# Attention with a routed expert layer: the gate's exponential, the third pair's decay rows, and the first pair's cast order

## The chip, the cores and the metric

The kernel runs on one core of a Trainium2 chip. The metric is the device time of one execution in microseconds (us). The engines are TensorE (PE, its weight load PEld), VectorE (DVE), ScalarE (ACT), GpSimd (POOL) and SyncE (SP, which issues most of the loads and stores). They run side by side, each through its own queue in order, and wait for each other by semaphores.

## What is computed

Causal attention with a decay per position for 8 batches of 8 heads (576 positions, 64 wide), whose output is sent through a layer of 8 experts, one for each token:

```
scores = scale * np.matmul(q, k.transpose(0, 1, 3, 2))
log_f = np.log(np.clip(f, 0.0001, 1.0))
cum = np.cumsum(log_f, axis=-1)
decay = cum[:, :, :, None] - cum[:, :, None, :]
scores = np.where(causal, -1000000000.0, scores + decay)
attn = np.exp(scores - scores.max(-1)) / sum
x = (attn @ v) as 4608 rows of 512
logits = x @ w_gate
expert_idx = np.argmax(logits, axis=1)
logits_shift = logits - logits.max(-1, keepdims=True)
probs = np.exp(logits_shift);  probs /= probs.sum(-1, keepdims=True)
out[token] = probs[expert_idx] * (relu(x @ w1[expert]) @ w2[expert])
```

## The kernel before

Attention works on pairs of heads: 32 pairs, numbered 0 to 31 here and in the code (n), four to a batch, so pair 0 is the first, pair 2 the third. A pair's q and k come as one tile of 128 partitions (two heads of q, then two of k: 1280 and 1152 columns), called `raw`. Every float is split into a rounded high part and the rest, and a score is a sum of two matmuls: the first multiplies the high parts (`qk1`, written qk in the profile), the second the rests together with the decay (`q2` and `k2`, 68 partitions; rows 64 to 67 hold the cumulated decay and constants). PE takes these two in that order for every tile, so a late `q2` or `k2` stops PE with the first matmul done.

The loop runs over n, and each n has seven steps i. In a step PE makes scores of pair n (`s_tiles`, `s_joint`), then transposes of the exponentials of pair n-1 (`t_tiles`, `t_one`, `t_joint`); in step 1 it also makes the products with v for pair n-2 (`av`). DVE reads each score bank, adds the mask and takes a row minimum (`s_red`, L339), ACT makes the exponential (`s_exp`, L346), and both copy transposes out of PSUM. The order of each engine's instructions is that of the loop (`order.pin`).

For pairs 0 and 1 the casts and splits are spread over ACT, DVE and POOL (`first_q`, `first_k`, `second_q`, `second_k`). From pair 2 on POOL does most of it: a cast of q, the rest of head 2's q (`q_parts`, in step 5 two pairs ahead), then a copy of q and the rest of k (`copies`, step 2 one pair ahead), four instructions in a row.

Loads are issued by SP in program order (`sp_dma`). A load's semaphore is one of eight, taken in turn, and the built program makes a load wait, where nothing later has done so, until the load eight places ahead of it has landed. The decay lies in the tile `cw` in SBUF. Pairs 0 and 1 get their decay rows straight from it (`c_rows`, five small transfers a pair); `cw` is also written to DRAM (`cq`, `ck`), and from pair 2 on the rows come from there (`load_c`, two transfers).

When a batch's four pairs are done, its routing runs between the steps of the next pairs. For batch b the logits are finished in pair 4b+6 (`fin_logits`, parts 0 and 1 in steps 3 and 4), and step 1 of pair 4b+7 runs `softmax` and `expert` (pairs 7, 11, up to 31): DVE takes the maximum and the shifted logits `w.sh`, which lie in the PSUM bank `ps_r` (pr in the profile), ACT takes their exponential (`ex`, L811), DVE compares them (`cand`, L814) and builds a one-hot table (`ohb`, L824), from which PE makes ranks in step 3 (L840). The last batch does the same while the first expert is under way. After attention comes the expert layer, a long run of matmuls (L1093, L1116).

Of the kernel before, what the change touches and what calls it, by code (L numbers as in the profile page):

```python
# [8 lines left out]
F32 = mybir.dt.float32  # L9
F32R = mybir.dt.float32r  # L10
# [3 lines left out]
AF = mybir.ActivationFunctionType  # L14
ALU = mybir.AluOpType
# [4 lines left out]
P = 128  # L20
S = 576
# [60 lines left out]
def psum(pool):  # L82
    return pool.tile([P, 512], F32, name="ps", tag="ps")
# [11 lines left out]
def attention_all(c, tc, qkT, va, vb, f, wgd, x_dram, batch_done, more_consts, extra):  # L95
# [6 lines left out]
    nc = tc.nc  # L102
    V = nc.vector
    B = qkT.shape[0]
    NH = B * H
    JW = S // 2
    QW = 1280
# [7 lines left out]
    with ExitStack() as st:  # L115
# [4 lines left out]
        sm, sp = c.sm, c.sp  # L120
# [18 lines left out]
        def sp_dma(out, in_):  # L139

            return tc.keep_in_program_order(nc.sync.dma_start(out, in_))

        def load_pair(n, parts=(0, 1)):

            if n not in raws:
                pool, tag = (c.xap, "xa") if n % 3 == 2 else (c.wp, "R")
                raws[n] = pool.tile([P, QW + 2 * S], F32, name="raw", tag=tag)
            raw = raws[n]
            b, p = divmod(n, NPAIR)
            cols = ((0, QW), (QW, QW + 2 * S)) if n < 3 else ((0, QW + 2 * S),)  # L150
            for c0, c1 in [cols[i] for i in parts if i < len(cols)]:
                for h in range(2):
                    last = sp_dma(raw[h * HD : (h + 1) * HD, c0:c1], qkT[b, p, :, c0:c1])
            return last
# [23 lines left out]
        halves = ((slice(0, NPR), slice(512, S)), (slice(NPR, NH), slice(S, 640)))  # L178
        for hs, cs in halves:
            scan(cum[hs, cs], fr[hs, 512:S], cum[hs, 511:512])  # L180
        cw = sp.tile([NH, 2, 640], F32R, name="cw", tag="aT")
        cwf = cw.bitcast(F32)
        V.tensor_copy(cw[:, 0, :], cum)
        V.tensor_tensor(cw[:, 1, :], cum, cwf[:, 0, :], ALU.subtract)
# [4 lines left out]
        NQ = 2  # L189
# [73 lines left out]
        def first_q(n):  # L263
            qk1, raw, q2 = operands(n), raws[n], Q2s[n]
            pin(nc.scalar.copy(qk1[:, 0:QW], raw[:, 0:QW]))
            if n == 1:
                nc.gpsimd.tensor_copy(q2[0:64], raw[0:64, 0:QW])

        def first_k(n):
            qk1, raw, q2 = ops[n][0], raws[n], Q2s[n]  # L270
            pin(nc.scalar.copy(qk1[:, QW:], raw[:, QW:]))  # L271
            if n == 0:
                pin(nc.scalar.copy(q2[0:64], raw[0:64, 0:QW]))

        def second_q(n):
            pin(lo(V, n, ops[n][0][64:128, 0:QW], 64, 0, QW))
# [30 lines left out]

        def c_rows(n, j):

            q2c, k2c = Q2s[n][64:66].bitcast(F32), K2s[n][66:68].bitcast(F32)  # L310
            r = cwf[j * NPR + n : j * NPR + n + 1]
            if j == 0:
                sp_dma(k2c[:, 0, :], r[:, :, 0:S])
                sp_dma(q2c[:, 0:640], r)
            else:
                sp_dma(k2c[:, 1, 0:512], r[:, :, 0:512])
                sp_dma(k2c[:, 1, 512:], r[:, :, S:640])
                sp_dma(q2c[:, 640:], r)
# [227 lines left out]
                    ))  # L546
                nc.scalar.copy(gT[:, q0:q1], g[:, 0 : q1 - q0])

        def fin_logits(b, part):
            rinv = rinvs[b]  # L550
            if part == 0:
                lgs[b] = (c.ps_r[:, 0:40].rearrange("p (t e) -> p t e", e=8),
                          sm.tile([P, 5, 8, 8], F32, name="gq", bufs=1))
            lg, gq = lgs[b]
            pg = psum(fin_bank[0])
            tiles = (0, 1, 2, 3) if part == 0 else (4,)
            for i, t in enumerate(tiles):
                note(nc.tensor.transpose(
                    pg[:, P * i : P * i + P], gT[:, P * t : P * t + P], c.ident
                ))  # L560
            for i, t in enumerate(tiles):
                V.tensor_tensor(
                    gq[:, t],
                    pg[:, P * i : P * i + P].rearrange("q (h e) -> q e h", e=16)[:, 0:8, :],
                    rinv[:, t, :].unsqueeze(1).to_broadcast([P, 8, 8]), ALU.mult,
                )
            if part == 1:
                V.tensor_reduce(lg, gq, AX.X, ALU.add)
# [4 lines left out]
        def fin_tasks(b):  # L573

            (softmax, expert, gate, rank, slot, hi, lo, table), after = batch_done(
                b, lambda: lgs[b][0]
            )
            fx = [lambda t=t: fin_x(b, t, b == B - 1 and t > 0) for t in range(5)]  # L580
            lg = [lambda p=p: fin_logits(b, p) for p in range(2)]
            g = NPAIR * b + 6
            if b == B - 1:
                return dict(fx=fx, lg=lg, softmax=softmax, expert=expert, gate=gate,
                            rank=rank, slot=slot, hi=hi, lo=lo, table=table,
                            logits=lambda: fin_gate(b))
            r = [(0, 2, fx[0]), (0, 3, lg[0]), (0, 4, lg[1]), (1, 1, softmax),
                 (1, 1, expert), (1, 3, rank)]
            if b < B - 2:
                r += [(2, 1, gate), (2, 1, slot), (2, 2, fx[1]), (2, 3, fx[2]),  # L590
                      (3, 1, hi), (3, 1, lo), (3, 2, fx[3]), (3, 3, fx[4]), (3, 5, table)]
            else:
                r += [(2, 1, gate), (2, 1, slot), (2, 2, fx[1]), (2, 3, hi), (2, 3, lo),
                      (2, 4, fx[2]), (2, 5, fx[3]), (2, 6, fx[4]), (3, 0, table)]
            for dn, i, f in r + after:
                tasks.setdefault((g + dn, i), []).append(f)
# [36 lines left out]
        c_rows(1, 0)  # L633
        c_rows(1, 1)
        load_pair(2)

        sp_dma(cq[:, :, 0], cwf[0:NPR])
        sp_dma(cq[:, :, 1], cwf[NPR:NH])
        sp_dma(ck[:, :, 0, :], cwf[0:NPR, :, 0:S])
        sp_dma(ck[:, :, 1, 0:512], cwf[NPR:NH, :, 0:512])  # L640
        sp_dma(ck[:, :, 1, 512:], cwf[NPR:NH, :, S:640])
        tasks, c.later, order = {}, [], InOrder(tc)
        c.note = note
        for n in range(NP + 2):
# [8 lines left out]
            for i in range(7):  # L653
                for x in c.later:
                    x[0] -= 1
                while c.later and c.later[0][0] <= 0:
                    c.later.pop(0)[1]()
                if n == 0:
                    if i == 0:
                        first_q(1)  # L660
                        late_consts()
                    elif i == 2:
                        second_q(1)
                    elif i == 3:
                        first_k(1)
                    elif i == 5:
                        second_k(1)
                elif n + 1 < NP:
                    if i == 0:
                        load_c(n + 1)  # L670
                        if n == 1:
                            load_pair(3)
                    elif i == 2:
                        copies(n + 1)
                if i == 5 and n + 2 < NP:
                    q_parts(n + 2)
                if i == 5 and n == 2:
                    load_gate()
                if i == 3 and n < NP:
                    load_v(n)  # L680
                if i == 2 and 0 < n < NP - 3:
                    c.mark = load_pair(n + 3)
                s_, e_ = ss[i] if ss else (None, None)
                if s_:
                    step(s_)
                if ts_:
                    step(ts_[i])

                if e_:
                    e_()  # L690
                if i == 1 and 0 < n and n + 1 < NP:
                    k_first(n + 1)
                if i == 1 and 2 <= n:
                    step(lambda: av(n - 2))
                    av_out()


                    fb, fp = divmod(n - 2, NPAIR)
                    if fp == 0 and 1 <= fb:
                        step(lambda: fin_gate(fb - 1))  # L700
                        fin_tasks(fb - 1)
                    elif fp == NPAIR - 1 and fb == B - 1:
                        todo = fin_tasks(fb)

                fin_bank[0] = (ps_v, ps_m)[i % 2]
                for f in tasks.pop((n, i), []):
                    step(f)
                at = {(0, 1): 0, (1, 0): 1, (1, 1 if b == B else 4): 2}.get((p, i))
                if n >= NPAIR and at is not None:
                    fin_sums(b - 1, at)  # L710
                if (n, i) == (NP, 0):
                    scores.close()
                for f in extra(n, i):
                    step(f)
                order.pin()
                if (n, i) == (NP + 1, 1):
                    break
# [12 lines left out]
E = 8  # L730
# [56 lines left out]
def route_stages(c, tc, b, lg_of, last):  # L787
# [14 lines left out]
    def softmax():  # L802
# [3 lines left out]
        w.sh = tokens(40, 5)  # L806
        V.tensor_tensor(w.sh, lg, bc(mx), ALU.subtract)

    def expert():
        w.ex = rs.tile([P, 5, E], F32, name="ex")  # L810
        nc.scalar.activation(w.ex, w.sh, AF.Exp)  # L811

        cand = rs.tile([P, 5, E], F32, name="cand")
        V.scalar_tensor_tensor(  # L814
# [606 lines left out]
```

## Time and profile before

| | |
|---|---|
| median of 3 runs | 862.28 us (861.4 to 862.44) |
| the profiled execution, time | 861.09 us |
| its span, first to last instruction | 859.3 us |
| PE busy | 816.6 us, 95% |
| DVE, ACT, POOL busy | 54%, 50%, 45% |
| mean granted clock of TensorE | 0.990 |

The profile gives, for one execution, each engine's busy time; a list of waits (which engine stood idle ahead of which line, and what released it); a timeline with starts and durations; and the busy time, granted clock and transfers in chosen stretches. Attention takes the span up to about 380 us, the experts the rest. An engine that isn't the one waited for may idle at no cost, so the waits of the busiest engine are read first.

### The profile page before, as it was taken

The page shows a single profiled execution, that of the slowest core. Times are in us where ns is not written, and L with a number is a line of the kernel's source. Part 1 is how long each engine was busy: PE and PEld are TensorE (multiplying, and loading weights), DVE is VectorE, ACT ScalarE, POOL GpSimd, SP SyncE. Part 2 cuts the span into 40 slices and gives each one's busy share as a digit, 9 for nine tenths or more (in the row PEclk, how much of TensorE's full clock was granted, in tenths as well). Part 3 has the DMA queues.
Part 4 walks back from the last instruction along what each step waited for, and adds up shares of the span by engine and source line. Part 5 has one row for each costly group of instructions (what it writes and reads, how often), then busy time and mean ns, then how long its engine had stood idle before and what let it go on. Part 6 is the DMA issues. An engine that isn't in the chain of part 4 may idle for free. (4 is left out here: it accounts for less than half of the span.)

```text
span 859.3 us, 15386 instructions
## 1 busy us (share of the span) xinstructions
PE 816.6 (95%) x5664; PEld 713.9 (83%) x5664; DVE 462.9 (54%) x1427; ACT 432.3 (50%) x1108; POOL 388.2 (45%) x310
## 2 busy tenths in 40 slices
PE   4899999999999999999999999999999999999992
PEld 3778787878787878788899899898898998988982
DVE  7656767676767778655472544445425444354200
ACT  6888888888888989855221223122122221231210
POOL 7798696969696978651530230312203103101010
PEclk9999999999999999999999999999999999999996
DMA  7997676767676765522651450533415405324000
GB/s 170 223 191 162 163 178 164 183 150 187 152 184 154 176 152 146 175 93 86 191 190 50 147 170 21 189 109 119 149 46 171 143 4 183 104 74 132 1 37 17
DMA packets 39893, 114.65 MB, mean 133 GB/s; under 512 B 6847, under 2 KB 8895, under 8 KB 36104
## 3 DMA queue, kind: packets, MB, share of 16 engines
q1 hardware_dynamic: 32776, 93.70, 42.2%
q0 software_dynamic: 6400, 19.93, 6.4%
q8 instruction: 46, 0.75, 0.4%
q14 instruction: 31, 0.25, 0.1%
q10 hardware_dynamic: 640, 0.01, 0.0%
HBM read 94.07 MB, written 20.55 MB: 133 GB/s over the span
## 5 line engine op out<-in xcount | busy, mean ns | idle before, releaser
L1116 PE MATMUL ps<-w,hh 128*128 128x512 f32 x640 | 199.3, 395 | 0.0
L346 ACT ACTIVATE sc<-sc,nmx 128x512 f32<-128x512 f32 (+4 forms) x288 | 167.3, 582 | 34.7 <-DVE nmx L339 34.2
L1124 POOL DMA_INDIRECT out<-y,si_fast x37 | 42.4, 1146 | 312.1 <-ACT y L1123 283.4
L339 DVE CUSTOM_DVE_ANT_0 sc<-ps,mask 128x512 f32<-128x512 f32 (+4 forms) x288 | 129.2, 479 | 63.7 <-PE ps L332 63.0
L1098 ACT ACTIVATE hh<-ps 128x384 fp32r<-128x384 f32 (+1 forms) x128 | 56.1, 438 | 194.5 <-PE ps L1093 194.5
L1093 PE MATMUL ps<-xa,w 128*128 128x384 f32 x768 | 145.1, 337 | 0.1
L332 PE MATMUL ps<-qk 128*128 128x288 f32 (+4 forms) x384 | 126.9, 361 | 16.0 <-ACT qk L271 10.8
L1099 DVE SCALAR_TENSOR_TENSOR hl<-ps,hh 128x384 fp32r<-128x384 f32 (+1 forms) x128 | 62.4, 489 | 146.2 <-ACT hh L1098 145.0
L1116 PEld LDWEIGHTS ps<-w,hh 128*128 128x128 f32 x640 | 118.2, 188 | 23.6
L1093 PEld LDWEIGHTS ps<-xa,w 128*128 128x128 f32 x768 | 132.7, 188 | 1.4 <-DVE hl L1099 0.2
L1116 PE MATMUL ps<-w,hl 128*128 128x512 f32 x320 | 124.8, 395 | 0.0
L332 PE MATMUL ps<-k,q 68*128 68x288 f32 (+4 forms) x384 | 105.7, 323 | 5.2 <-POOL k L249 3.8
L249 POOL TENSOR_TENSOR k<-raw,qk 64x1152 fp32r<-64x1152 f32 x30 | 79.4, 2647 | 53.7 <-ACT qk L291 49.0
L1093 PE MATMUL ps<-xb,w 128*128 128x256 f32 x768 | 101.8, 283 | 0.0
L1093 PEld LDWEIGHTS ps<-xb,w 128*128 128x128 f32 x768 | 98.9, 189 | 2.8
L470 PE MATMUL ps<-aT,va_t 128*64 128x256 f32 (+3 forms) x896 | 94.6, 354 | 0.0
L1123 ACT ACTIVATE y<-ps,g_fast 128x512 f32<-128x512 f32 x37 | 25.5, 689 | 136.6 <-PE ps L1116 130.7
L391 ACT COPY aT<-ps 128x512 f32<-128x512 f32 (+1 forms) x156 | 83.2, 534 | 14.1 <-PE ps L400 6.8
L332 PEld LDWEIGHTS ps<-qk 128*128 128x128 f32 x384 | 69.6, 195 | 23.6 <-ACT qk L271 10.8
L249 POOL TENSOR_TENSOR qk<-raw,qk 64x1280 fp32r<-64x1280 f32 x30 | 87.8, 2928 | 2.4
L470 PEld LDWEIGHTS ps<-aT,va_t 128*64 128x64 f32 x896 | 58.9, 137 | 29.2 <-issue 6.1
L969 DVE CAST w<-wraw 128x1024 fp32r<-128x1024 f32 x56 | 39.2, 707 | 80.3 <-PE ps L1116 54.3
(161 smaller groups left out, 1133.2 us busy)
## 6 DMA issues: line engine op xcount, KB each, us to landing
raw<-in_qkT SPq DMA_DIRECT2D x58, 608.0 KB
wraw<-in_w SPq DMA_DIRECT2D x63, 512.0 KB
va_t<-in_va SPq DMA_DIRECT2D x32, 256.0 KB
x_dram<-row SPq DMA_DIRECT2D x32, 256.0 KB
raw<-in_qkT SPq DMA_DIRECT2D x6, 320.0 KB
raw<-in_qkT SPq DMA_DIRECT2D x6, 288.0 KB
vb<-in_vb SPq DMA_DIRECT2D x32, 32.0 KB
x_dram<-row SPq DMA_DIRECT2D x8, 128.0 KB
```

What stands on the lines that cost most here:

```text
L249: return eng.tensor_tensor(o, raws[n][p0 : p0 + 64, c0:c1], ops[n][0][p0 : p0 + 64, c0:c1].bitcast(F32), ALU.subtract,)
L332: note(nc.tensor.matmul(out, ql[:, q0 : q0 + P], kl[:, j, k0 : k0 + kw], start=(i == 0), stop=(i == last),))
L339: V.tensor_tensor_reduce(scs[n][:, dst : dst + src.shape[1]], src, m, -0.125, init, ALU.add, ALU.min, nms[n][:, col : col + 1],)
L346: nc.scalar.activation(x, x, AF.Exp, bias=nms[n][:, col : col + 1], scale=-1.0, accum_out=acc)
L391: nc.scalar.copy(dst, src)
L470: c.last_av = note(nc.tensor.matmul(pv[j * HD : (j + 1) * HD, q0 - qa : qb - qa], l, r, start=(blk == 0), stop=(blk == nb - 1),))
L969: V.tensor_copy(w[:, 0], raw)
L1093: c.note(nc.tensor.matmul(ph[:, 0:n], w[:, wi, fs], x[:, xi, kt, :], start=(k == 0), stop=(k == 3 * KT - 1),))
L1098: nc.scalar.activation(hh[:, ft, :], ph[:, 0:n], AF.Relu)
L1099: nc.vector.scalar_tensor_tensor(hl[:, ft, :], ph[:, 0:n], 0.0, hh[:, ft, :].bitcast(F32), ALU.max, ALU.subtract,)
L1116: c.note(nc.tensor.matmul(py, hi_[:, ft, ms], w[:, wi], start=(ft + k == 0), stop=(ft == FT - 1 and k == 2),))
L1124: nc.gpsimd.indirect_dma_start(out=self.out, out_offset=bass.IndirectOffsetOnAxis(ap=si[:, s : s + 1], axis=0), in_=y, in_offset=None, bou ...
```

## The change

There are four edits.

1. Gate. `softmax` subtracts the maximum a second time, into a new SBUF tile `shs`, and ACT's exponential reads that in place of `w.sh` in PSUM. Part 1 of `fin_logits` moves from step 4 of pair 4b+6 to step 0 of pair 4b+7 and takes the bank `ps_m`. This is done for batches 0 to 6; the last batch gets the second subtraction alone.
2. Pair 2's decay rows come straight from `cw`, as those of pairs 0 and 1, and are issued ahead of pair 3's raw data; the writes to `cq` and `ck` come behind that. `cw` is taken from the pool of `xT`.
3. Pair 2's raw data is loaded whole, in two transfers in place of four.
4. Pair 0's `q2` cast goes ahead of its k cast on ACT, and the k casts of pairs 0 and 1 are made in two halves of 576 columns.

```diff
-            cols = ((0, QW), (QW, QW + 2 * S)) if n < 3 else ((0, QW + 2 * S),)
+            cols = ((0, QW), (QW, QW + 2 * S)) if n < 2 else ((0, QW + 2 * S),)
...
-        cw = sp.tile([NH, 2, 640], F32R, name="cw", tag="aT")
+        cw = c.xp.tile([NH, 2, 640], F32R, name="cw", tag="xT")
...
             pin(nc.scalar.copy(qk1[:, 0:QW], raw[:, 0:QW]))
-            if n == 1:
-                nc.gpsimd.tensor_copy(q2[0:64], raw[0:64, 0:QW])
...
-            pin(nc.scalar.copy(qk1[:, QW:], raw[:, QW:]))
             if n == 0:
                 pin(nc.scalar.copy(q2[0:64], raw[0:64, 0:QW]))
+            else:
+                nc.gpsimd.tensor_copy(q2[0:64], raw[0:64, 0:QW])
+
+        def first_k(n):
+            qk1, raw = ops[n][0], raws[n]
+            for c0, c1 in ((QW, QW + S), (QW + S, QW + 2 * S)):
+                pin(nc.scalar.copy(qk1[:, c0:c1], raw[:, c0:c1]))
...
-            r = [(0, 2, fx[0]), (0, 3, lg[0]), (0, 4, lg[1]), (1, 1, softmax),
+            r = [(0, 2, fx[0]), (0, 3, lg[0]), (1, 0, lambda: fin_logits(b, 1, ps_m)), (1, 1, softmax),
                  (1, 1, expert), (1, 3, rank)]
...
                 elif n + 1 < NP:
-                    if i == 0:
+                    if i == 0 and n > 1:
                         load_c(n + 1)
-                        if n == 1:
-                            load_pair(3)
+                    elif i == 0:
+                        c_rows(2, 0)
+                        c_rows(2, 1)
+                        load_pair(3)
+                        c_writes()
...
         V.tensor_tensor(w.sh, lg, bc(mx), ALU.subtract)
 
+        w.shs = rs.tile([P, 5, E], F32, name="shs")
+        V.tensor_tensor(w.shs, lg, bc(mx), ALU.subtract)
...
-        nc.scalar.activation(w.ex, w.sh, AF.Exp)
+        nc.scalar.activation(w.ex, w.shs, AF.Exp)
```

On DVE, from the end of pair 6 to the maximum in pair 7's step 1, before (ISA rows are `s_red`, gq and pr<-gq are part 1 of the logits, mx the maximum; the subtraction and `cand` follow):

```order
L562 TENSOR_TENSOR gq<-ps,rinv 128x64
L568 TENSOR_REDUCE pr<-gq 128x40
L339 ISA sc,nmx<-ps,mask 128x288
L339 ISA nmx 128x1
L389 COPY aT<-ps 68x2x64
L339 ISA sc,nmx<-ps,maskj,nmx 128x288
L339 ISA nmx 128x1
L339 ISA sc,nmx<-ps,mask 128x512
L339 ISA nmx 128x1
L339 ISA sc,nmx<-ps,mask 128x512
L339 ISA nmx 128x1
L805 TENSOR_REDUCE mx<-pr 128x5
```

The same place on DVE in the changed kernel:

```order
L341 ISA sc,nmx<-ps,mask 128x512
L341 ISA nmx 128x1
L564 TENSOR_TENSOR gq<-ps,rinv 128x64
L570 TENSOR_REDUCE pr<-gq 128x40
L341 ISA sc,nmx<-ps,mask 128x512
L341 ISA nmx 128x1
L811 TENSOR_REDUCE mx<-pr 128x5
L813 TENSOR_TENSOR pr<-pr,mx 128x40
L816 TENSOR_TENSOR shs<-pr,mx 128x40
L823 SCALAR_TENSOR_TENSOR cand<-pr,iota5m 128x40
```

Part 1 of the logits has moved behind the first `s_red` of pair 7, and one subtraction stands ahead of `cand`; everything behind keeps its order.

On SP's queue, from pair 2's raw data on, before (q and k with cw or cq, ck are decay rows):

```order
L141 DMA raw<-in_qkT 64x1280 x2
L141 DMA raw<-in_qkT 64x1152 x2
L141 DMA cq<-cw 64x1x640 x2
L141 DMA ck<-cw 64x1x576
L141 DMA ck<-cw 64x1x512
L141 DMA ck<-cw 64x1x64
L141 DMA va_t<-in_va 128x512
L141 DMA vb_174<-in_vb 64x128
L141 DMA q_0_142<-cq 2x1280
L141 DMA k_0_144<-ck 2x1152
L141 DMA raw<-in_qkT 64x2432 x4
```

The same stretch of SP's queue in the changed kernel, whose next rows are the rest of ck and pair 4's raw data:

```order
L141 DMA raw<-in_qkT 64x2432 x2
L141 DMA va_t<-in_va 128x512
L141 DMA vb_174<-in_vb 64x128
L141 DMA k_0_144<-cw 2x1x576
L141 DMA q_0_142<-cw 2x1x640
L141 DMA k_0_144<-cw 2x1x512
L141 DMA k_0_144<-cw 2x1x64
L141 DMA q_0_142<-cw 2x1x640
L141 DMA raw<-in_qkT 64x2432 x2
L141 DMA cq<-cw 64x1x640 x2
L141 DMA ck<-cw 64x1x576
```

Pair 2's raw data is two rows in place of four, the five writes to DRAM stand behind pair 3's raw data and ahead of pair 4's, and the rows of pair 2 no longer come through DRAM.

## Rows read from the trace of the kernel before

**Rows 1.** The page, busy time of PE, share and instructions.

```profile
PE 816.6 (95%) x5664; PEld 713.9 (83%) x5664; DVE 462.9 (54%) x1427; ACT 432.3 (50%) x1108; POOL 388.2 (45%) x310
```

**Rows 2.** Waits of PE, whole span: who <- released by: us, times, longest.

```profile
PE ps L332 <- ACT qk L271: 10.8, 1, 10.8
PE ps L332 <- DVE nmx L339: 4.5, 7, 0.7
PE ps L332 <- POOL k L249: 3.8, 2, 2.6
PE pr L840 <- DVE ohb L824: 2.7, 6, 0.4
PE ps L400 <- DVE aT L389: 1.9, 1, 1.9
...
PE ps L332 <- DMA q<-cw: 1.4, 1, 1.4
```

**Rows 3.** PE in a stretch: from:to, length, busy, granted clock, transfers' share, GB/s.

```profile
60.00:360.00 300.00, 292.17 (x2534) 1.00 0.69 166
```

**Rows 4.** Waits of DVE, whole span.

```profile
DVE cand L814 <- ACT ex L811: 24.5, 8, 3.5
```

**Rows 5.** Timeline, pair 7: start, us, engine line operation [idle before <- releaser].

```profile
88.99 0.34 PE L332 MATMUL ps<-k,q 68*128 68x384 f32 x1
...
89.88 0.22 ACT L811 ACTIVATE ex<-pr 128x40 f32<-128x40 f32 x1
...
90.13 0.20 DVE L814 SCALAR_TENSOR_TENSOR cand<-pr,iota5m 128x40 f32<-128x40 f32 x1 [3.47 <-ACT ex L811]
...
91.25 0.55 DVE L339 CUSTOM_DVE_ANT_0 sc<-ps,mask 128x384 f32<-128x384 f32 x1
...
91.39 0.20 PE L840 MATMUL pr<-ohb,trib 128*128 128x48 bf16 x1 [0.44 <-DVE ohb L824]
...
95.27 0.47 PE L332 MATMUL ps<-qk 128*128 128x512 f32 x1 [0.71 <-DVE nmx L339]
```

**Rows 6.** Timeline, pair 31, the seventh batch routed.

```profile
359.74 0.62 ACT L346 ACTIVATE sc<-sc,nmx 128x384 f32<-128x384 f32 x1 [1.26 <-DVE nmx L339]
...
361.71 0.29 DVE L389 COPY aT<-ps 128x128 f32<-128x128 f32 x1 [0.91 <-ACT aT L391]
...
364.02 0.69 DVE L389 COPY aT<-ps 128x512 f32<-128x512 f32 x1
...
364.76 1.00 PE L400 MATMUL ps<-ident,sc 128*128 128x128 f32 x4 [1.94 <-DVE aT L389]
```

**Rows 7.** PE in two stretches, columns as in rows 3.

```profile
364.00:369.00 5.00, 4.24 (x24) 0.66 0.02 5
39.00:43.00 4.00, 1.41 (x10) 1.00 1.06 228
```

**Rows 8.** Timeline of ACT and PE, pair 0.

```profile
10.62 1.25 ACT L273 CAST q<-raw 64x1280 fp32r<-64x1280 f32 x1
...
10.76 0.80 PE L332 MATMUL ps<-qk 128*128 128x512 f32 x1 [10.76 <-ACT qk L271]
...
12.92 0.77 PE L332 MATMUL ps<-k,q 68*128 68x512 f32 x1 [1.36 <-DMA q<-cw]
```

**Rows 9.** Timeline of POOL: its first instructions for pairs 2 and 3.

```profile
21.55 1.25 POOL L287 CAST qk<-raw 128x1280 fp32r<-128x1280 f32 x1 [3.47 <-DMA raw<-in_qkT]
...
33.86 1.25 POOL L287 CAST qk<-raw 128x1280 fp32r<-128x1280 f32 x1 [4.12 <-DMA raw<-in_qkT]
```

**Rows 10.** Timeline of PE: the second matmul of pairs 2 and 3.

```profile
29.80 0.50 PE L332 MATMUL ps<-k,q 68*128 68x512 f32 x1 [1.25 <-POOL k L249]
...
42.05 0.50 PE L332 MATMUL ps<-k,q 68*128 68x512 f32 x1 [2.60 <-POOL k L249]
```

**Rows 11.** Timeline of SP's queue: raw data of pairs 2, and 3 with 4.

```profile
16.10 2.44 SPq L141 DMA_DIRECT2D raw<-in_qkT  x4
...
25.72 2.43 SPq L141 DMA_DIRECT2D raw<-in_qkT  x4
```

More of the change, by code (lines that the diff above doesn't have):

```diff
@@ L265, in first_q @@
             pin(nc.scalar.copy(qk1[:, 0:QW], raw[:, 0:QW]))
-            if n == 1:
+            if n == 0:
+                pin(nc.scalar.copy(q2[0:64], raw[0:64, 0:QW]))
+            else:
                 nc.gpsimd.tensor_copy(q2[0:64], raw[0:64, 0:QW])
         def first_k(n):
-            qk1, raw, q2 = ops[n][0], raws[n], Q2s[n]
-            pin(nc.scalar.copy(qk1[:, QW:], raw[:, QW:]))
-            if n == 0:
-                pin(nc.scalar.copy(q2[0:64], raw[0:64, 0:QW]))
+            qk1, raw = ops[n][0], raws[n]
+            for c0, c1 in ((QW, QW + S), (QW + S, QW + 2 * S)):
+                pin(nc.scalar.copy(qk1[:, c0:c1], raw[:, c0:c1]))
         def second_q(n):
@@ L308, in c_rows @@
         def c_rows(n, j):
-            q2c, k2c = Q2s[n][64:66].bitcast(F32), K2s[n][66:68].bitcast(F32)
+            q2c, k2c = (t[n % NQ][r : r + 2].bitcast(F32) for t, r in ((Q2s, 64), (K2s, 66)))
             r = cwf[j * NPR + n : j * NPR + n + 1]
@@ L547, in fin_gate, with fin_logits @@
                 nc.scalar.copy(gT[:, q0:q1], g[:, 0 : q1 - q0])
-        def fin_logits(b, part):
+        def fin_logits(b, part, bank=None):
             rinv = rinvs[b]
@@ L554, in fin_logits @@
             lg, gq = lgs[b]
-            pg = psum(fin_bank[0])
+            pg = psum(bank or fin_bank[0])
             tiles = (0, 1, 2, 3) if part == 0 else (4,)
@@ L635, in attention_all, with c_writes @@
         load_pair(2)
[L637 to L641, printed above, removed]
+        def c_writes():
+            sp_dma(cq[:, :, 0], cwf[0:NPR])
+            sp_dma(cq[:, :, 1], cwf[NPR:NH])
+            sp_dma(ck[:, :, 0, :], cwf[0:NPR, :, 0:S])
+            sp_dma(ck[:, :, 1, 0:512], cwf[NPR:NH, :, 0:512])
+            sp_dma(ck[:, :, 1, 512:], cwf[NPR:NH, :, S:640])
         tasks, c.later, order = {}, [], InOrder(tc)
@@ L681, in attention_all @@
                 if i == 2 and 0 < n < NP - 3:
-                    c.mark = load_pair(n + 3)
+                    load_pair(n + 3)
                 s_, e_ = ss[i] if ss else (None, None)
```

## The prediction

> **What bounds the kernel now.** I read the page first: PE is busy 816.6 us [rows 1] of a span of 859.3, so time can only be won where PE stands idle, and the list of PE's waits says where that is. Of the 43 us of idle time, 10.8 lie ahead of the first matmul, 1.4 behind it, 3.8 are waits for POOL's `k2`, and the rest of what is listed are waits for DVE: 4.5 us for score minima, 2.7 for the one-hot table, 1.9 for a transpose copy [rows 2]. A stretch that leaves out start and end confirms it: from 60 to 360 us PE is busy 292.2 of 300 us, at a granted clock of 1.00 (2.4 GHz), so 7.8 us is all that can be won there by removing waits [rows 3]. The list of DVE's waits then names what makes DVE late: `cand` waits for ACT's `ex` 24.5 us in 8 waits of up to 3.5 us, in the pairs 7, 11 to 31 and after the last batch [rows 4]. Both instructions only read the tile in PSUM. DVE has nothing to wait for in its own data; it waits because the built program orders it behind ACT's read.
>
> **The gate, six batches.** In pair 7 DVE stands idle 3.47 us up to 90.13, when ACT has reached `ex` at 89.88, behind its other work of that step; the one-hot table follows, and only at 91.25 does DVE take the score bank that PE had finished with the matmul of 88.99 to 89.33. PE waits 0.44 us for the table and, three steps later, 0.71 us for a bank that DVE has not read yet [rows 5]. With `shs` in SBUF, `cand` has no wait for ACT in the built program, so DVE can do `cand` and the table from 86.7 on (90.13 less 3.47), all of it inside the idle 3.47 us, and is ready for the bank at 89.4, some 1.8 us sooner. That is more than 0.44 and 0.71. ACT's copies, behind which DVE waits in the next two steps, take their turn after DVE's minima and move up with them. The second subtraction is one more DVE instruction of the size of `cand`, 0.20 us [rows 5], and part 1 of the logits, moved by one step, is no more work; both lie in what was idle. PE's transpose for it stands a few instructions later in a queue that runs on. What is late next is nothing on DVE: it then waits for PE. So the six table waits, 2.7 us, and six of the seven waits for minima, 4.3 us (the seventh lies in pair 0), should go [rows 2]. With the smaller stops between them the ceiling is the 7.8 us of [rows 3]; I take **-7.3 us**.
>
> **The gate, seventh batch.** Pair 31 holds more work on DVE and ACT, and the stop there is larger. ACT waits 1.26 us for a minimum at 359.74, DVE waits for ACT's copy until 361.71, does its last copy of the step at 364.02, and PE, which waited 1.94 us, goes on at 364.76 [rows 6]. Without the stall ACT's exponential starts at once, so this chain moves up by its 1.26 us, and PE's wait shrinks to some 0.7 us: -1.3 us. The gap has a second price. From 364 to 369 us the granted clock is 0.66 on the mean [rows 7], which is 3.4 us at the lower level (1.2 GHz) and the rest at the upper, after PE had stood idle. Five us at 0.66 lose 1.7 us of PE's work; some of it is the idle time itself, so 1.5 us. A gap of 0.7 us leaves the clock alone, as the 0.71 us waits did in [rows 3]. Together **-2.8 us**; bounds 0 (the gap stays) and -3.6 (gap and clock loss both vanish).
>
> **First pair.** ACT's `q2` cast, now behind the k cast, takes 1.25 us from 10.62; the first matmul starts at 10.76, but the second waits until 12.92 for the decay rows, which have their own transfer [rows 8]. Their place in SP's queue does not change. With `q2` first and half of k behind it PE may start some 0.5 us earlier and then waits that much longer. The second halves of the k casts cost at most another instruction's start on ACT; what hides them is this wait and, behind it, the wait of pair 2. **0 us**; if the cover were gone, -0.5.
>
> **Pair 2, the third.** POOL starts on it at 21.55, when the two transfers with its q have landed, and on pair 3 at 33.86 [rows 9]. PE's second matmul of pair 2 starts at 29.80 after a wait of 1.25 us for POOL, 8.2 us after POOL's start, and that of pair 3 at 42.05 after 2.60 us [rows 10]. Now POOL's first cast waits for whole transfers with q and k. How late these land the trace shows for the same form: pair 3's were issued from 25.72 on [rows 11] and POOL began at 33.86, 8.1 us later. Pair 2's are issued from 16.10 on [rows 11], so POOL begins near 24.2, **2.7 us later than before**, and PE's second matmul of pair 2 starts near 32.4. The bounds are 23 (the second half of the bytes at a faster rate) and 25. The decay rows, five small transfers, go out when PE has done with pair 0 near 20 us, far ahead of 32.4.
>
> Pair 3 gains what pair 2 loses. In the built program its raw data waits until the first half of the eight loads ahead, pair 2's raw data, has landed, and so is issued near 24.2 rather than 25.72, when the decay rows had come back from DRAM; in 8.1 us it is there, at 32.4, just when POOL is done with pair 2. POOL then needs another 8.2 us, to 40.6. PE needs 9.65 us from the second matmul of pair 2 to its stop in pair 3 (29.80 to 42.05 less 2.60 [rows 10]) and so comes to pair 3 at 42.1: no wait is left, and PE is where it was, at 42.05. The 2.60 us wait of pair 3 has become a longer wait of pair 2: **+0.1 us**. The rows of pair 3 still come through DRAM, behind writes that now stand behind its raw data; the bytes ahead of them are the same, and the loads don't stand idle as long for them, so they should land ahead of 42; up to 1.5 us is the bound if they don't. The moved writes also stand ahead of pair 4's raw data, which POOL wants at 40.6 in place of 42.
>
> **The longer gap.** PE then stands idle 1.25 + 2.7 = 3.9 us ahead of 32.4. After 2.60 us of idling the granted clock was 1.00 (39 to 43 us), after 1.94 us it fell [rows 7]. So a gap's length alone does not decide, but 3.9 us is longer than either, and I expect the fall to the lower level: a price between 0 and 1.7 us, and I take **+1.4**, near the row where it fell, as part of the low stretch may lie in the gap. The Trainium skill, page "TensorE: Matmul & The Clock Gate", section "Part 1: The HAM clock gate", says that half rate is the default that activity lifts, and that the check is "free-running — it doesn't reset when your kernel starts". By this rule one and the same gap can cost or not from run to run, and the sum would be 1.4 us better in some runs; the two gaps of [rows 7] agree with it.
>
> **Sum.** -7.3 - 2.8 + 0 + 0.1 + 1.4 = -8.6 us. Against the profiled execution (861.09 us) that is 852.5. The median is 1.2 us above that execution, so I forecast **853.7 us**.
>
> **Rivals.**
> The clock does not fall after the longer gap. For it: it didn't after 2.60 us. Against: this gap is half as long again. 862.28 - 10.0 = 852.3 us.
> The waits go by half. DVE is free earlier, but the waits for minima three steps later stay, since ACT's copies hold DVE up there (0.91 us in [rows 6]). For it: that wait is there in the row. Against: ACT itself waits for DVE 2 us ahead of it, and moves up when DVE does. 4.3 us stay: 858.0 us.
> The change doesn't do what it says: `cand` gets another late wait, DVE stalls as before, and only pair 2's cost is left, 862.28 + 1.5 = 863.8 us. Against it stands the built order, in which `cand` follows the two subtractions on its own engine with no wait for ACT.
> The loads become the bound, and the kernel is slower. From 39 to 43 us the transfers' share is 1.06 and PE waits [rows 7]; SP now stands at the small rows of pair 2 until PE releases them, and later at pair 3's rows until the DRAM writes have landed. If the loads then stand idle for longer than they do before by X, each pair to about 60 us comes later by X. The decision point is X = 10.3 us, where -8.6 + 10.3 passes +1.7; at 12 us the time is 865.7. Against it: eight loads are under way at a time, and the longest wait for a load in [rows 9] is 4.12 us.
>
> **How the numbers follow.** The forecast has 0.50 (853.7), the unchanged clock 0.25 (852.3), half the waits 0.13 (858.0), no effect 0.04 (863.8), the loads 0.02 (865.7), and 0.06 is left for gains beyond my ceiling, near 850. A measurement of this kernel tells 0.2%, 1.7 us, from no change. Faster: 0.50 + 0.25 + 0.13 + 0.06 = 0.94; same 0.04; slower 0.02. The range goes from 851.0 (no clock loss, all of the 7.8 us) to 858.0.
>
> **What would show it.** `cand` with no wait for ACT; no idle time of PE ahead of the ranks and of step 0 of pairs 8, 12 up to 28; from 60 to 360 us PE busy to within 1 us of the stretch; a gap near 0.7 us in pair 31 at a clock of 1.00; POOL's first cast of pair 2 near 24.2, PE's wait ahead of pair 2 near 3.9 us with a low clock behind it, none ahead of pair 3. I am wrong if pair 3 still waits for POOL or its rows, or if the stops in pairs 7 to 31 only move.

## The result and the profile after

| | before | after |
|---|---|---|
| median | 862.31 us (861.4 to 862.44) | 849.28 us (848.61 to 850.01) |
| ratio | | 0.9851, 95% interval 0.9834 to 0.9868 |
| profiled execution, time and span | 861.09, 859.3 us | 850.01, 848.3 us |
| mean granted clock | 0.990 | 0.987 |

The change saves 13.0 us where 8.6 were forecast. 849.28 lies below the range (851.0 to 858.0), in the case that had 0.06, gains beyond the ceiling.

The first line of the page of after, beside [rows 1]:

```profile
PE 812.9 (96%) x5664; PEld 715.0 (84%) x5664; DVE 464.3 (55%) x1435; ACT 432.9 (51%) x1110; POOL 391.7 (46%) x310
```

PE executes the same 5664 matmuls and is busy 3.7 us less, although its clock was a little lower. That already says that "busy" held something other than work. The list of PE's waits in after (who, released by: us in total, times, longest), beside [rows 2]:

```profile
PE ps L334 <- POOL k L250: 3.3, 1, 3.3
PE ps L334 <- POOL qk L250: 2.0, 1, 2.0
PE ps L334 <- DMA q<-cw: 1.6, 1, 1.6
PE ps L402 <- DVE aT L391: 1.0, 1, 1.0
...
PE ps L334 <- DVE nmx L341: 0.3, 1, 0.3
```

The table waits (2.7 us in 6) are gone, those for minima are down from 4.5 us in 7 to one of 0.3. DVE's 24.5 us of waiting for `ex` [rows 4] are gone too. Pair 7 in after, DVE and ACT, beside [rows 5]:

```profile
89.42 0.19 DVE L823 SCALAR_TENSOR_TENSOR cand<-pr,iota5m 128x40 f32<-128x40 f32 x1
...
90.40 0.21 DVE L833 CAST ohb<-pr 128x48 bf16<-128x48 f32 x1
91.83 0.56 DVE L341 CUSTOM_DVE_ANT_0 sc<-ps,mask 128x384 f32<-128x384 f32 x1 [1.22 <-PE ps L334]
...
91.83 0.25 ACT L820 ACTIVATE ex<-shs 128x40 f32<-128x40 f32 x1
```

`cand` and the table follow the subtractions at once, 2.4 us ahead of ACT's exponential, and DVE then waits 1.22 us for PE: it has changed from late to early.

**Where the time went**, from the starts of pairs in the timelines. From pair 6's start to pair 31's, PE does the same 2365 matmuls in both kernels. These are that stretch of before and of after (from:to, length, PE busy, granted clock, transfers' share, GB/s):

```profile
71.78:351.44 279.66, 271.99 (x2365) 1.00 0.68 164
```

```profile
74.39:342.87 268.48, 268.05 (x2365) 1.00 0.71 171
```

The stretch is 11.18 us shorter. What follows pair 31's start is 2.43 us shorter (859.3 - 351.44 = 507.86, and 848.3 - 342.87 = 505.43); 2.39 of it lies ahead of the first expert matmul, 19.93 us behind that start in before and 17.54 in after. What comes ahead of pair 6 is 2.61 us longer in these two executions. The sum, -11.0, is the difference of the spans. The medians differ by 13.0, since the execution of before lay 1.2 us under its median and that of after 0.7 over. By medians the start therefore costs what is left, 13.6 less 13.0, some +0.6 us, which is within the noise of the medians.

### The profile page after: what moved, and what is told of

Same layout as the page of the kernel before. It is cut to its first block, busy times and chain, and to the rows that moved or that the text cites. A ratio compares the mean times of both kernels' runs of the same rounds, so it can differ in the third digit from the quotient of the medians.

```text
span 848.3 us, 15393 instructions
## 1 busy us (share of the span) xinstructions
PE 812.9 (96%) x5664; PEld 715.0 (84%) x5664; DVE 464.3 (55%) x1435; ACT 432.9 (51%) x1110; POOL 391.7 (46%) x310
## 3 DMA queue, kind: packets, MB, share of 16 engines
q0 software_dynamic: 6400, 19.93, 6.4%
```

## The experiments

Medians are of 4 to 10 runs; each was compared with runs of the kernel before on the same chip, whose medians were 861.8 to 862.5. Theory L says that the gate brought the whole gain, since PE's stops were longer than listed, and that the start costs; theory P, that the gate brought what was forecast and the start the rest.

**The gate alone, and the start alone.** g_only is the kernel before with edit 1; start_only is the kernel after without it:

```diff
-            r = [(0, 2, fx[0]), (0, 3, lg[0]), (0, 4, lg[1]), (1, 1, softmax),
+            r = [(0, 2, fx[0]), (0, 3, lg[0]), (1, 0, lambda: fin_logits(b, 1, ps_m)), (1, 1, softmax),
...
+        w.shs = rs.tile([P, 5, E], F32, name="shs")
+        V.tensor_tensor(w.shs, lg, bc(mx), ALU.subtract)
...
-        nc.scalar.activation(w.ex, w.sh, AF.Exp)
+        nc.scalar.activation(w.ex, w.shs, AF.Exp)
```

> The kernel before with the gate's edit alone (shs in SBUF, part 1 of the logits moved); loads, decay rows and casts of the start as before. Theory L (the gate is worth more than the idle time listed ahead of its waits, because that idle time is counted from a modelled end of the matmul ahead; the start's edits cost time): pair 7 takes 10.1 us as in the changed kernel (11.75 before), attention's start as before with pair 3's second matmul near 42.05, and the time is 862.3 - 13.7 = 848.6 us. Theory P (as predicted, the gate is worth 10.1 us, and the other 3 us come from the start's edits): 852.2 us.

> The changed kernel with the gate's edit undone: only the start's edits (pair 2 loaded whole, its decay rows from SBUF ahead of pair 3's raw data, cast order). Theory L: pair 3's second matmul near 46.5 as in the changed kernel, half of that won back in pair 4, where the wait of 1.2 us behind ACT's small transfer goes; 862.3 + 2.6 = 864.9 us. Theory P: 859.3 us.

g_only: 848.37 us (847.46 to 848.86), ratio 0.9839 (0.9823 to 0.9856). start_only: 862.61 us, ratio 1.0001 (0.9991 to 1.001). The gate brings all of it, as L said. Its time is 0.9 us under that of the whole change, though the intervals of the two ratios overlap. For start_only both theories missed: the three start edits together, alone, move nothing that can be measured.

The same stretch as above in g_only:

```profile
73.47:341.92 268.45, 268.03 (x2365) 1.00 0.72 171
```

It is the stretch of after to within 0.03 us: nothing of the start reaches behind pair 6.

**The two halves of the gate.** shs_only has the second subtraction and the exponential from SBUF (the last two pieces of the diff above), lg_only the moved logits (the first piece).

> The kernel before with shs in SBUF alone; part 1 of the logits stays in step 4 of the pair before. Theory L: the stops ahead of the ranks and behind them go, and the short stop in step 1 of pair 7 (the next score matmul 0.68 us behind the start of the transposes, 0.46 in the changed kernel) stays: 0.2 us for each of six batches less than with both, 850.0 us. Theory P: 852.4 us.

> The kernel before with the logits edit alone (the fifth transpose of the gate's logits into the next step's own bank); the exponential still reads the logits' bank. Theory A (the two edits of the gate remove different stops, so their gains add: both together 14.0, the exponential's alone 11.8): 2.2 us less than before, 859.9 to 860.5. Theory B (both act on the one wait for the logits' bank, which the exponential still holds): within 0.8 us of 862.3.

shs_only: 850.55 us, ratio 0.9867 (0.9851 to 0.9884), -11.8 us; near L's 850.0. lg_only: 857.62 us, ratio 0.9953 (0.9936 to 0.997), -4.2 us, which neither theory had. The two gains alone add up to 16, both together bring 13.9. From pair 6's start to pair 31's, which leaves the start's differences out, shs_only wins 9.0 us (279.66 to 270.62), lg_only 4.0 (to 275.64) and both together 11.2, 1.8 less than the sum. The two kernels share part of one stop, and the timelines show which. PE in pair 7 of shs_only, then of lg_only:

```profile
90.92 0.63 PE L400 MATMUL ps<-ident,sc 128*128 128x128 f32 x4
91.38 0.19 PE L843 MATMUL pr<-ohb,trib 128*128 128x48 bf16 x1
...
93.73 0.60 PE L430 MATMUL ps<-ident,sc 128*128 128x128 f32 x4
94.41 0.47 PE L332 MATMUL ps<-qk 128*128 128x512 f32 x1
```

```profile
89.06 0.62 PE L400 MATMUL ps<-ident,sc 128*128 128x128 f32 x4
89.82 0.20 PE L840 MATMUL pr<-ohb,trib 128*128 128x48 bf16 x1
...
92.37 0.60 PE L430 MATMUL ps<-ident,sc 128*128 128x128 f32 x4
93.70 0.47 PE L332 MATMUL ps<-qk 128*128 128x512 f32 x1 [0.73 <-DVE nmx L339]
```

From the transposes to the table's matmul it is 1.06 us in before, 0.76 with the logits moved, and 0.46 with the exponential from SBUF. So either edit wins the same 0.30 us there, 1.8 us in six batches. The stop ahead of the next pair goes with the exponential's edit alone (1.33 us from start to start with the logits moved, 0.68 with the exponential's edit).

**The start's edits, one by one.** whole_only loads pair 2 in two transfers (the diff's first line alone); casts_only has the new cast order; rows_only pair 2's rows from `cw` ahead of pair 3's raw data, and the writes behind.

> The kernel before with one edit: the third pair's raw data (pair 2) in two transfers, not four. Theory A (the order of the whole start decides; the forecast's own term): POOL's first cast of that pair begins near 24.2 us, where it was 21.55 with four transfers, the second matmul of the pair is near 32.4, and the time is within 1 us of 862.3. Theory B (the two large transfers are slower by themselves, whatever lies between): POOL begins at 25.5 us or later, as the 25.66 of the changed kernel, with a stop of about 3 us ahead of the pair's second matmul; the clock then falls, and the time is 863 to 865.

> The kernel before with one edit: the casts of the first two pairs in the new order (ACT's copy of the first pair's k in two, its q2 ahead of k). Theory A: first matmul within 0.4 us of 10.76, second within 0.2 us of 12.92, since q's rows by DMA land last; time 861.5 to 863. Theory B (ACT was on the path): second matmul at 12.3 or earlier, and the time 0.5 us or more below 862.3.

> The kernel before with the decay rows' edits alone: pair 2's rows from SBUF, pair 3's raw data and the DRAM writes behind them; transfers and casts as before. Theory A (no start edit is worth anything alone, since every version stops about 5 us in pairs 2 and 3 and pair 6 begins at 72 to 74.4): within 1 us of 862.3. Theory B (the decay rows cost what the whole start lost on top of the gate, since pair 3's k rows come later through DRAM): a stop over 3 us at pair 3's second matmul for k<-ck, and 863.2 to 864.

862.34 us, ratio 0.9995 (0.9985 to 1.0004); 862.46 us, 0.9998 (0.9989 to 1.0008); 860.32 us, 0.9988 (0.9972 to 1.0003), with runs from 858.5 to 864.5. No edit alone is worth anything that can be measured. Of the expectations, whole_only has A's time with B's stop and fallen clock. casts_only has A's time, but its first two matmuls, at 10.19 and 12.63 us, lie somewhat earlier than A's bounds. rows_only has B's stop of over 3 us (3.63, for k<-ck), while its time lies 2 us below A's 862.3 and so misses both. In whole_only POOL begins, and PE makes the second matmul of pair 2, at

```profile
24.94 1.25 POOL L287 CAST qk<-raw 128x1280 fp32r<-128x1280 f32 x1 [6.54 <-DMA raw<-in_qkT]
```

```profile
33.14 0.79 PE L332 MATMUL ps<-k,q 68*128 68x512 f32 x1 [3.39 <-POOL k L249]
```

That lies between the two expectations: of the 4.1 us by which POOL begins later in after (25.66, 21.55 in [rows 9]), 3.4 come with the two large transfers alone and 0.7 with the other start edits. The small rows that now go out beside the transfers may be the reason for the 0.7; no run separates them from the casts.

**Whole transfers or four, in the kernel after.**

```diff
-            cols = ((0, QW), (QW, QW + 2 * S)) if n < 2 else ((0, QW + 2 * S),)
+            cols = ((0, QW), (QW, QW + 2 * S)) if n < 3 else ((0, QW + 2 * S),)
```

> The changed kernel with pair 2's raw data in four transfers again (q first, then k). Theory L: POOL begins pair 2 near 21.8 in place of 25.7, the gap ahead of its second matmul shrinks to under 2 us, the granted clock stays at 1.00, and the time is 849.3 - 3 = 846 to 847 us. Theory P (the start's edits are what won the rest): loading it in halves brings nothing or loses, 849.3 us or more.

849.81 us, ratio 0.9858 (0.9842 to 0.9875): L's 846 to 847 was a miss, and P's 849.3 or more came. Pair 2's second matmul comes 3.8 us earlier (30.08, not 33.85), and pair 3 gives it back:

```profile
43.18 0.77 PE L334 MATMUL ps<-k,q 68*128 68x512 f32 x1 [3.44 <-DMA k<-ck]
```

Pair 3's decay rows, which still pass through DRAM, are now what PE waits for.

**Three other orders of the start, with the gate.** early3 issues pair 3's raw data right behind pair 2's; rows3 takes pair 3's rows from SBUF too and puts the writes a pair later; early3b is rows3 with pair 3's raw data ahead of pair 2's rows. The core of early3b against the kernel after (transfers and casts as before):

```diff
-                    if i == 0 and n > 1:
+                    if i == 0 and n > 2:
                         load_c(n + 1)
                     elif i == 0:
-                        c_rows(2, 0)
-                        c_rows(2, 1)
-                        load_pair(3)
-                        c_writes()
+                        c_rows(n + 1, 0)
+                        c_rows(n + 1, 1)
+                        if n == 2:
+                            c_writes()
...
                 if i == 3 and n < NP:
                     load_v(n)
+                    if n == 0:
+                        load_pair(3)
```

> Gate as in the changed kernel; at the start pair 2 in four transfers again, pair 3's raw data right behind them, pair 2's decay rows from SBUF, and all DRAM writes of the decay rows behind those; casts as before. Theory A (the start's loss is only the order in which loads land): the stop ahead of pair 3's second matmul (2.9 to 3.4 us in the two kernels that had the gate and four transfers) shrinks under 1.5 us, the clock stays at 1.00 behind it, pair 6 begins near 71.5 instead of 73.5 to 74.4, and the time is 845.5 to 847. Theory B (whatever is moved at the start, the gap goes to the next pair, since bytes and not their order set it): a stop near 3 us remains in pair 2 or pair 3, the clock falls, pair 6 begins at 73.5 or later, time 848 to 850.

> Gate as in the changed kernel; at the start pair 2 in four transfers with casts as before, pair 2's and pair 3's decay rows both from SBUF, pair 3's raw data right behind pair 2's rows, and the DRAM writes of the decay rows a whole pair later. Theory A (the start's loss is the order in which loads land, and the late row that stopped pair 3 in the other kernels is one that came through DRAM): the stop ahead of pair 3's second matmul, 2.9 to 3.4 us so far, falls under 1.5 us, pair 6 begins by 72.0, and the time is 846 to 847.5 against 848.4 of the gate alone. Theory B (bytes set it, or the stop in pair 2 alone keeps the clock low): pair 6 begins at 73.0 or later as in every kernel with the gate alone, time 848 to 850.

> Gate as in the changed kernel; pair 2 in four transfers, pair 3's raw data issued right behind pair 0's v, ahead of the decay rows of pair 2; pair 2's and pair 3's rows from SBUF, the DRAM writes behind pair 3's rows. Theory A (the start's stops come from POOL's idle time ahead of pair 3, 4.2 us from its last work on pair 2 to the landing of pair 3's raw data): POOL begins pair 3 within 1.5 us of finishing pair 2, near 30 to 31.5 us instead of 34.2, the stop at pair 3's second matmul goes, one stop of 1 to 2 us stays in pair 2, pair 6 begins by 71.0, and the time is 845 to 846.5. Theory B (a stop always remains, as in the six versions so far, and the clock falls behind it): pair 6 begins at 73 or later, 848 to 850.

851.08 us (ratio 0.9873), 850.21 us (0.9866), 848.53 us (0.9841, 0.9825 to 0.9858); none beats the gate alone. The first two went the way of their theory B, with times 1.1 and 0.2 us above its 850. In early3b POOL begins pair 3 at 31.89 instead of 34.2, pair 3's stop is gone as theory A said, and the time isn't: the stop of pair 2 has grown to 2.55 us, since its q row now queues behind that raw data, the clock falls behind it, and a stop of 1.31 us that after had lost is back in pair 4. PE in early3b, and its stretch behind the first stop:

```profile
31.78 0.47 PE L333 MATMUL ps<-k,q 68*128 68x512 f32 x1 [2.55 <-DMA q<-cw]
```

```profile
32.00:36.00 4.00, 4.00 (x19) 0.57 0.96 201
```

All versions side by side (stops of PE by the timeline, the lowest granted clock in 4-us slices from 28 to 52 us, and pair 6's start; one execution each, us):

| kernel | pair 2 | pair 3 | pair 4 | lowest clock | pair 6 starts |
|---|---|---|---|---|---|
| before | 1.25 | 2.60 | 1.16 | 1.00 | 71.78 |
| after | 1.99 + 3.28 | none | none | 0.50 | 74.39 |
| start_only | 2.51 + 3.09 | none | none | 0.50 | 73.96 |
| g_only | 1.02 | 2.87 | none | 0.50 | 73.47 |
| shs_only | none | 3.02 | none | 0.65 | 72.38 |
| lg_only | 1.72 | 1.09 | 0.23 | 0.74 | 70.84 |
| whole_only | 0.18 + 3.39 | none | none | 0.52 | 73.30 |
| casts_only | 1.93 | 2.14 | 1.28 | 0.66 | 72.93 |
| rows_only | 1.11 | 3.63 | none | 0.57 | 72.75 |
| halves | 2.29 | 3.44 | none | 0.50 | 74.07 |
| early3 | 2.33 | 2.45 | none | 0.57 | 74.50 |
| rows3 | 1.14 | 2.68 | 0.32 | 0.50 | 74.22 |
| early3b | 2.55 | none | 1.31 | 0.57 | 72.64 |
| g_rank5 | 0.83 | 2.95 | none | 0.77 | 71.98 |

The stops move from one pair to another, and 3.0 to 5.7 us of them stay in every version. At least one stop is followed by a low clock in all but the profiled execution of before. Five of these kernels (before, g_only, shs_only, lg_only, g_rank5) are the same program up to pair 6 and yet reach it between 70.84 and 73.47 us. So 2.6 us of the last column come from one execution to the next, and the table can't rank the orders of the start.

**The rank two steps later.** A stop of 0.31 us is left in after ahead of pair 8's first matmul (0.67 us from start to start, where 0.36 is usual), and DVE's four rank operations stand ahead of the bank read there.

```diff
-                 (1, 1, expert), (1, 3, rank)]
+                 (1, 1, expert), (1, 5, rank)]
```

> The kernel before with both edits of the gate, and the rank task (four VectorE operations) two steps later, from step 3 to step 5 of its pair. Theory A (the stop of about 0.3 us ahead of each eighth pair's first matmul, seen from start to start, comes from VectorE's bank read behind those four operations): 0.2 to 0.3 us less at each of six batches, time 846.5 to 847.3 against 848.4 of the gate alone. Theory B (that stop is not VectorE's order; the later rank delays the slot and table work behind it): time 848.4 or more.

847.67 us (846.96 to 848.45), ratio 0.9832 (0.9816 to 0.9849). The stop goes, and its place shows in the rows, but the next pair takes it back:

```profile
93.02 0.60 PE L430 MATMUL ps<-ident,sc 128*128 128x128 f32 x4
93.38 0.48 PE L332 MATMUL ps<-qk 128*128 128x512 f32 x1
...
99.79 0.44 PE L508 MATMUL ps<-ident,xT 128*128 128x128 f32 x2 [0.31 <-ACT xT L479]
```

Pair 7 takes 9.76 us instead of 10.07, pair 8 10.80 instead of 10.53. From pair 6 to pair 31 that is 268.23 against 268.45: 0.2 us, not 1.8. The profiled executions differ by 1.7 us (848.86 and 847.18), of which 1.5 lie ahead of pair 6, which the edit doesn't touch. The medians differ by 0.7, and the intervals overlap. Theory A had the cause of the stop and not its worth. This and g_only are the fastest versions measured, 0.9 (g_only) and 1.6 us (g_rank5) below the kernel after, though the intervals of the ratios overlap with its own.

## Why the prediction was wrong, point by point

**The gate, six batches: the mechanism held, the term was mis-sized.** The forecast was -7.3 us under a ceiling of 7.8; it was -11.18. The step that failed is "7.8 us is all that can be won there by removing waits" [rows 3], with the -7.3 drawn from it. Listed idle time in the stretch fell from 7.67 us (279.66 - 271.99) to 0.43, by 7.24: that is the forecast almost exactly. The other 3.94 us came out of "busy" time, 271.99 against 268.05 us for the same 2365 matmuls at a clock of 1.00. A matmul's end on the page is modelled, so a stop behind it is listed only from the modelled end on. The page of the profile says that the ends are modelled, and the Trainium skill, page "Perfetto Trace Analysis", section "Tensor Engine Instruction (MATMUL, LD_WEIGHTS)", says it as a rule: "the TE profile time is a model, not a measurement". The trace agrees, with 3.94 us; the prediction had drawn nothing from either. In the rows of g_rank5 above, four transposes are listed with 0.60 us, while the next matmul starts 0.36 us behind their start (93.02 and 93.38). A stop there has to be longer than the difference, 0.24 us, to be listed at all.

Before, the rows of the weight loads had shown it. Pair 7 of before, PE and PEld:

```profile
84.08 0.60 PE L400 MATMUL ps<-ident,sc 128*128 128x128 f32 x4
...
84.73 0.19 PEld L332 LDWEIGHTS ps<-qk 128*128 128x128 f32 x1 [0.29 <-PE ps L400]
84.76 0.48 PE L332 MATMUL ps<-qk 128*128 128x512 f32 x1
...
90.33 0.62 PE L400 MATMUL ps<-ident,sc 128*128 128x128 f32 x4
91.39 0.10 PEld L840 LDWEIGHTS <-trib 128*128 128x128 bf16 x1 [0.68 <-DVE ohb L824]
...
92.00 0.28 PE L332 MATMUL ps<-k,q 68*128 68x256 f32 x1
92.28 0.42 PEld L419 LDWEIGHTS ps<-ident,sc 128*128 128x128 f32 x4 [0.20 <-DVE aT L389]
...
93.95 0.60 PE L430 MATMUL ps<-ident,sc 128*128 128x128 f32 x4
```

The same places in after:

```profile
86.58 0.60 PE L402 MATMUL ps<-ident,sc 128*128 128x128 f32 x4
...
87.04 0.48 PE L334 MATMUL ps<-qk 128*128 128x512 f32 x1
...
92.62 0.62 PE L402 MATMUL ps<-ident,sc 128*128 128x128 f32 x4
93.08 0.19 PE L849 MATMUL pr<-ohb,trib 128*128 128x48 bf16 x1
...
95.43 0.60 PE L432 MATMUL ps<-ident,sc 128*128 128x128 f32 x4
96.10 0.47 PE L334 MATMUL ps<-qk 128*128 128x512 f32 x1
```

From start to start, where no modelled end enters: ahead of step 1's scores 0.68 and 0.46 us (PE lists no wait; PEld lists 0.29; in after the moved logits' transpose stands in between); ahead of the table 1.06 and 0.46 (0.60, where PE lists 0.44 and PEld 0.68); ahead of the joint step's transposes 0.28 and 0.12, and behind them 0.41 and 0.36 (nothing listed on PE, 0.20 on PEld); ahead of the next pair 1.32 and 0.67. That is 1.68 us a batch, where 1.15 was listed. Pair 6 and its like lose another 0.11, the logits' part that moved. Six batches make 10.1 us, seven pairs like pair 6 another 0.8, and pair 24 is 0.3 shorter (10.88 and 10.54): that is the 11.18. The list of PEld's waits in before, whole span:

```profile
PEld L840 <- DVE ohb L824: 4.3, 7, 0.7
PEld ps L400 <- DVE aT L389: 3.8, 8, 2.2
PEld ps L419 <- DVE aT L389: 2.8, 8, 1.4
...
PEld ps L332 <- PE ps L400: 2.1, 7, 0.4
```

Against PE's own 2.7 for the table and 1.9 for the copy [rows 2], and 1.2 in one wait at L419, these lines hold the longer and the unlisted stops.

The rival "the waits go by half" was wrong for the reason that the prediction gave: ACT moved up with DVE, and the minima are no longer late. Gains beyond the ceiling, 0.06 of the chances, were the case that came. The prediction's lower end, 851.0, is described there as no clock loss and all of the 7.8 us. By the prediction's terms these two give 851.8; 851.0 takes the seventh batch's bound of -3.6 as well.

**The gate, seventh batch: right, -2.4 for -2.8.** The gap in pair 31 shrank from 1.94 us to 0.95 (forecast 0.7), and the clock behind it stayed at 1.00, as forecast, where it was 0.66 [rows 7]:

```profile
354.54 0.66 PE L402 MATMUL ps<-ident,sc 128*128 128x128 f32 x4 [0.95 <-DVE aT L391]
```

```profile
354.00:364.00 10.00, 9.06 (x74) 1.00 0.07 26
```

**First pair: right, 0.** The second matmul still waits for the decay rows (12.80 us, before 12.92 in [rows 8]); casts_only is at 0.9998.

**Pair 2, the third: the way was right, the times were late.** POOL begins at 25.66 (forecast 24.2, bound 25), the second matmul of pair 2 is at 33.85 (32.4), and pair 3 waits no more, as forecast:

```profile
25.66 1.26 POOL L289 CAST qk<-raw 128x1280 fp32r<-128x1280 f32 x1 [7.56 <-DMA raw<-in_qkT]
```

```profile
29.96 0.60 PE L334 MATMUL ps<-qk 128*128 128x512 f32 x1 [1.99 <-POOL qk L250]
33.85 0.79 PE L334 MATMUL ps<-k,q 68*128 68x512 f32 x1 [3.28 <-POOL k L250]
```

The 8.1 us from issue to landing, taken from pair 3, were 9.6 here. PE is not where it was: pair 3's second matmul comes at 46.49, where 42.05 was forecast. Of these 4.4 us, 1.4 are the later second matmul of pair 2 (4.05 us later, for the 2.60 us that pair 3 no longer waits), and 3.0 are the slower way from there to pair 3 (12.64 us in place of 9.65), at the low clock.

**The longer gap: it fell, and cost more.** The forecast had one gap of 3.9 us ahead of the second matmul. There were two, since the first matmul of pair 2 waited for POOL as well: 1.99 and 3.28 us, 5.27 together. The clock fell behind the first of them, not behind the long one. It is low for some 10 us:

```profile
26.00:31.00 5.00, 2.58 (x18) 0.92 0.86 195
31.00:40.00 9.00, 6.15 (x25) 0.50 1.00 248
40.00:44.00 4.00, 4.00 (x39) 0.94 1.08 231
```

A mean of 0.92 over 5 us is 0.8 us at the lower level, and 0.94 over 4 us is 0.5.

PE goes on at 33.85, so up to 40 us 6.2 us of its work ran at half speed: 3.1 us, nearly twice the bound of 1.7, which came from the shorter low stretch of [rows 7]. Yet by medians the start costs only some +0.6 us (+0.9 against g_only), and the profiled executions are 2.61 us apart at pair 6. Pair 4 pays for a part: it takes 9.41 us instead of 10.88, because a stop of 1.16 us is gone that the prediction had not looked at. In before, ACT stood until 58.59 for its small transfer and DVE's copy came late:

```profile
58.59 0.51 ACTq L492 DMA_DIRECT2D js<-jsum  x1
...
60.00 0.66 PE L419 MATMUL ps<-ident,sc 128*128 128x128 f32 x4 [1.16 <-DVE aT L389]
```

In after the same transfer goes out at 60.61 and ACT doesn't stand still for it. By the built program it waits for the load eight places ahead of it; that this load is what held it in before is likely, and no row names it. Part of the clock's price was probably also counted twice. The prediction charged 1.4 us against a profiled execution in which the clock had not fallen, and then added the 1.2 us by which the median lies above it. All five kernels with before's transfers and rows at the start (g_only, shs_only, lg_only, casts_only, g_rank5) show a fall in their profiles. That agrees with a fall in most runs of before, and is not proof of it. Over 52 runs of before, the 17 with a mean clock of 0.990 or more have a median of 861.7 us, the 21 of 0.988 or less 862.8.

**The sum, corrected:** 853.7 - 3.9 (the hidden part of the stops) + 0.4 (seventh batch) - 0.9 (the start, +0.6 for +1.5) = 849.3 us; measured 849.28. The start's term is what the other two leave of the difference, so this sum closes by construction. Measured by itself the start is not clear of noise: +0.9 us against g_only, +0.3 in start_only (862.61 and 862.32). Which order of the start would leave PE no stop stays open: none of the versions had it.

## What to carry to other kernels

Idle time listed for TensorE is a lower bound, and span less "busy" is no ceiling: measure a stop from start to start of its matmuls, against the same place in a pair that runs undisturbed, or read the weight loads' waits, before sizing what removing it brings. Two engines that only read one PSUM tile can cost each other more than the tile's own work; here a second copy in SBUF (0.2 us on an idle engine) took away 24.5 us of VectorE's waiting. At a start bound by loads, a transfer moved forward moves another back, and an edit there should be judged by when the first undisturbed pair begins, in several executions, not by the stop that it removes.

## What the runs showed of the hardware

Behind pair 31 in before the clock stayed at the lower level for 3.4 us, and so it did behind the stops of lg_only, casts_only and early3b. Behind that of g_only it stayed there for some 7 us, in after for some 10. Whether it fell at all did not go by the stop's length alone: it fell behind stops of 1.72 (lg_only), 1.93 (casts_only) and 1.99 us (after), not behind 2.14 (pair 3 of casts_only), 2.29 (halves) or 2.60 (before), and again behind 2.55 (early3b) and 2.87 (g_only). That fits the rule that the prediction took from the Trainium skill, page "TensorE: Matmul & The Clock Gate", section "Part 1: The HAM clock gate": a check that runs free of what the kernel does lets one and the same gap cost or not.

In g_only the low stretch follows the stop in pair 3:

```profile
42.52 0.80 PE L332 MATMUL ps<-k,q 68*128 68x512 f32 x1 [2.87 <-POOL k L249]
```

```profile
44.00:48.00 4.00, 4.00 (x19) 0.50 1.08 205
```

The matmul right behind the stop takes 0.80 us, where the same one behind 1.25 us of idling took 0.50 [rows 10].
